# Dynamic convolution into a two-layer tanh-shrink network: a softmax product on another engine, another way of filling the halo and the weights, and another last superblock

## Chip, core and metric

The kernel runs on one core of one Trainium2 chip. The metric is the device time of one execution in microseconds (us), as the median of several runs. The engines are named as in the profile: PE (matmuls), PEld (its weight loads), DVE (vector), ACT (scalar, activations), POOL (GpSimd), SP (issues DMAs).

## What is computed

```python
# x: 8 x 4096 x 192, weight_gen: 8 x 4096 x 8 heads x 7 taps
w = np.exp(weight_gen - max over taps);  w = w / sum over taps
x_pad = six zero rows ahead of each sequence, then x
conv[b, s, h, g] = sum over k of w[b, s, h, k] * x_pad[b, s + k, h, g]    # 24 channels per head
h = conv.reshape(32768, 192) @ w_in        # 192 x 2048
g = h - np.tanh(h)
out = g @ w_out                            # 2048 x 192
```

## The kernel before

The 32768 tokens are cut into 32 superblocks of 1024 tokens, four to a sequence; a superblock puts 8 consecutive tokens (`J`) on each of the 128 partitions. For superblock n the stages are these.

`load(n)` (lines 71 to 105) issues the DMAs on SP: the taps `wg_t`, and `x_t`, which holds for each partition its 8 rows and the 6 rows ahead of them (the halo). In the first superblock of a sequence the halo of partition 0 is zero: DVE writes it with a memset (line 94), and the rows come in three DMAs rather than one.

`softmax_exp(n)` is one ACT instruction (line 110), `e_t`. `softmax_norm(n)` is three on DVE: the sum over taps `zsum` (120), its reciprocal `zr` (124), and the product `wsm` = `e_t` * `zr` (126, 448 elements per partition).

`products(n)` (133) makes seven tiles `prod0` to `prod6`, one per tap, each `x_t` shifted by the tap times that tap's weight (1536 elements per partition). They are on POOL, save in the first two superblocks: DVE makes taps 1, 3, 5, 6 of superblock 0 and taps 2, 5 of superblock 1. Each tap has two buffers.

`conv(n, chunks)` (151) sums the seven products and transposes them, with 64-row matmuls against an identity into `pc`; ACT copies the result to `convT` (174). It is called twice, for channel chunks 0 and 1 and for chunk 2.

`gemm1(n, f)` (182), for each of 16 tiles of the 2048 hidden columns, makes `ph` in PSUM with 12 half-array matmuls per pair of tiles; ACT takes `th` = tanh(`ph`) (196); DVE takes `gt` = `ph` - `th` (198). `ph` and `pc` share three PSUM buffers of two banks each.

`gemm2(i)` (204) makes the output of token block i (8 blocks to a superblock): 16 matmuls on the upper 64 rows of the array for block i and 16 on the lower 64 rows for block i-1, in turns, so that the two halves of one block's sum are made in two successive calls and add up in one bank, `po`. ACT copies `po` to `out_sb` (242); a superblock's output leaves in one DMA.

The order of the program is written out by hand (lines 251 to 297), and every engine runs its own instructions in that order. `w_in` is wanted twice, on partitions 0 to 63 and on 64 to 127: before, 16 DMAs on POOL's queue read it twice from memory (256), then one reads `w_out` (261). Then come the softmax and the products of superblocks 0 and 1, and a loop over n: `products(n+2)`, `load(n+3)`, and for p = 0 to 7 two calls of `gemm1(n)`, one of `gemm2` for superblock n-1, `conv(n+1)` at p = 2 and p = 5, `softmax_exp(n+3)` at p = 1 and `softmax_norm(n+3)` at p = 2. The last trip, n = 32, holds only the `gemm2` calls of superblock 31, and one more call closes the last block.

Of the kernel before, what the change touches and what calls it, by code (L numbers as in the profile page):

```python
# [16 lines left out]
def kernel(  # L17
# [42 lines left out]
    make_identity(nc, ident[:])  # L60

# [3 lines left out]
    wsm_of = {}  # L65
# [5 lines left out]
    def load(n):  # L71
# [21 lines left out]
        if s == 0:  # L93
            nc.vector.memzero(x_t[0:1, 0:HALO, :])  # L94
# [22 lines left out]
    def softmax_norm(n):  # L117
# [6 lines left out]
        nc.vector.reciprocal(zr[:], zsum[:])  # L124
        wsm = wgpool.tile([P, J, H, K], FP32, name="wsm")
        nc.vector.tensor_mul(  # L126
# [4 lines left out]
        wsm_of[n] = wsm  # L131

    def products(n, on_vector=()):
        x_t = x_of.pop(n)
        wsm = wsm_of.pop(n)
# [64 lines left out]

    half = {}
    out_of = {}

    def gemm2(i):

        ops = []
        for r, blk in ((0, i), (1, i - 1)):
            if not 0 <= blk < NTOT * J:
                continue
            n, j = divmod(blk, J)  # L210
            if r == 0:
                half[blk] = psum_o.tile([P, 512], FP32, name="po")
            ops.append((r, n, j, half[blk]))
        for f in range(NFT):
            for r, n, j, po in ops:
# [8 lines left out]
                if r == 1 and f == 0 and i in (1, NTOT * J):  # L224
# [26 lines left out]
    load(0)  # L251

    w_in = const.tile([P, NC, F], BF16, name="w_in")
    for r in range(2):
        for h in range(H):
            nc.gpsimd.dma_start(  # L256
                out=w_in[r * R + h * GC : r * R + (h + 1) * GC],
                in_=moe_w_in[h * G : (h + 1) * G].rearrange("(c g) f -> g c f", c=NC),
            )
    w_out = const.tile([P, NFT, D], BF16, name="w_out")  # L260
    nc.gpsimd.dma_start(out=w_out[:], in_=moe_w_out.rearrange("(c p) e -> p c e", c=NFT))  # L261

    ctx.enter_context(tc.manual_schedule())
# [7 lines left out]
    load(2)  # L271
    conv(0, (0, 1))
    conv(0, (2,))
    products(1, on_vector=(2, 5))
    softmax_exp(2)
    softmax_norm(2)
    for n in range(NTOT + 1):
        if n + 2 < NTOT:
            products(n + 2)
        if n + 3 < NTOT:  # L280
            load(n + 3)
        for p in range(J):
            if n < NTOT:
                gemm1(n, 2 * p)
                gemm1(n, 2 * p + 1)
# [4 lines left out]
            if n + 1 < NTOT:  # L290
                if p == 2:
                    conv(n + 1, (0, 1))
                if p == 5:
                    conv(n + 1, (2,))
            if p == 2 and n + 3 < NTOT:
                softmax_norm(n + 3)
    gemm2(NTOT * J)
# [30 lines left out]
```

## Time and profile before

| what | value |
|---|---|
| median of 3 runs | 861.99 us (861.54 to 863.34) |
| the profiled execution | 862.46 us |
| its span | 860.7 us, so 1.76 us lie around it |
| mean granted clock of PE | 0.984 |
| busy: PE, DVE, ACT, POOL | 779.2, 707.5, 641.3, 644.9 us |

A row of the timeline has a start, a duration, the engine, the line, what is written and read, how many instructions it merges (x4), and in brackets how long the engine was idle before it and who ended that. A row of the windows has a stretch, its length, each engine's busy time (with the number of instructions), the granted clock of PE, the busy share of the DMA engines and GB/s.

### The profile page before, as it was taken

The numbers are of one execution on the slowest core, as the hardware profiler recorded it, in microseconds if no ns is written. First come the engines' busy times: TensorE is split into PE (matmuls) and PEld (weight loads), VectorE is DVE, ScalarE is ACT, GpSimd is POOL, SyncE is SP. The second block draws the span as 40 slices with busy tenths as digits, with TensorE's granted clock in tenths as the row PEclk, the third lists the DMA queues.
The fourth block names the chain that finished last, engine by engine and source line by source line (L and its number), as shares of the span: only waits on it lengthen the run. The fifth ranks groups of instructions, "written<-read, shape, count | busy, mean of one in ns | idle before, by whom it ended". The sixth has DMA issues, their size and how long they took to land.

```text
span 860.7 us, 36095 instructions
## 1 busy us (share of the span) xinstructions
PE 779.2 (91%) x16640; PEld 604.4 (70%) x16640; DVE 707.5 (82%) x622; ACT 641.3 (75%) x865; POOL 644.9 (75%) x241
## 2 busy tenths in 40 slices
PE   0337999989999899999999899998999899999996
PEld 0224877767777677777777677776777677777775
DVE  4397888898888888888888988888888978887790
ACT  1136888868888688878788788887888678888881
POOL 3899888878888688986888699886888788884000
PEclk9978999999999999999999999999999999999999
DMA  9822223331333232233223322332233313200111
GB/s 197 146 77 76 88 93 114 114 113 50 114 115 93 86 115 83 81 115 113 84 97 114 113 64 102 113 114 77 104 113 115 113 51 113 104 11 30 40 39 75
DMA packets 17192, 81.19 MB, mean 94 GB/s; under 512 B 4368, under 2 KB 8464, under 8 KB 12952
## 3 DMA queue, kind: packets, MB, share of 16 engines
q1 hardware_dynamic: 13952, 76.52, 26.8%
q0 software_dynamic: 3088, 2.36, 2.1%
q8 instruction: 130, 2.13, 1.0%
q14 instruction: 22, 0.18, 0.1%
HBM read 56.06 MB, written 25.17 MB: 94 GB/s over the span
## 4 chain that ended last, share of the span: by engine, by line
PE 66%; DVE 21%; ACT 7%; issue 2%; DMA 2%; POOL 2%; DVEq 0%; POOLq 0%
PE po L217 31%; PE ph L187 31%; DVE gt L198 15%; ACT th L196 6%; PE pc L164 4%; DVE wsm L126 4%; DMA w_in<-in_moe_w_in_dram 2%; POOL prod L141 1%; DVE zr L124 1%; DVE zsum L120 1%; POOL w_in L256 1%; ACT out_sb L242 1%; DVE x_t L94 0%; ACT e_t L110 0%; POOL ident masks.py:199 0%
## 5 line engine op out<-in xcount | busy, mean ns | idle before, releaser
L141 POOL TENSOR_TENSOR prod<-x_t,wsm 128x1536 bf16<-128x1536 f32 x218 | 633.6, 2943 | 122.4 <-PE pc L164 121.7
L198 DVE TENSOR_TENSOR gt<-ph,th 128x1024 bf16<-128x1024 f32 x512 | 600.7, 1217 | 101.5 <-ACT th L196 101.3
L196 ACT ACTIVATE th<-ph 128x1024 f32<-128x1024 f32 x512 | 498.2, 1022 | 81.7 <-PE ph L187 79.3
L187 PE MATMUL ph<-convT,w_in 64*128 64x512 bf16 x3072 | 397.1, 381 | 35.4 <-DVE gt L198 31.7
L217 PEld LDWEIGHTS <-gt 64*128 64x128 bf16 x8192 | 359.2, 95 | 57.7 <-issue 5.7
L217 PE MATMUL po<-w_out,gt 64*128 64x192 bf16 x8192 | 390.6, 244 | 4.8 <-ACT out_sb L242 3.8
L187 PEld LDWEIGHTS <-w_in 64*128 64x128 bf16 x3072 | 169.3, 95 | 155.6 <-issue 63.2
L164 PE MATMUL pc<-ident,prod 64*128 64x64 bf16 x5376 | 93.7, 192 | 36.8 <-POOL prod L141 35.0
L164 PEld LDWEIGHTS <-prod 64*128 64x128 bf16 x5376 | 89.8, 96 | 38.2 <-POOL prod L141 35.3
L242 ACT ACTIVATE out_sb<-po 128x192 f32<-128x192 f32 x256 | 85.2, 333 | 39.7 <-PE po L217 36.2
L174 ACT ACTIVATE convT<-pc 128x1024 bf16<-128x1024 f32 x64 | 51.8, 810 | 79.8 <-PE pc L164 79.6
L126 DVE TENSOR_TENSOR wsm<-e_t,zr 128x448 f32<-128x448 f32 x32 | 56.2, 1756 | 2.7
L120 DVE TENSOR_REDUCE zsum<-e_t 128x64 f32<-128x448 f32 x32 | 19.5, 609 | 15.7 <-ACT e_t L110 15.7
L110 ACT ACTIVATE e_t<-wg_t 128x448 f32<-128x448 f32 x32 | 18.4, 575 | 13.4 <-DMA wg_t<-in_weight_gen_dram 13.4
L256 POOL DMA_DIRECT2D w_in<-in_moe_w_in_dram x16 | 9.4, 592 | 15.1 <-DMA w_in<-in_moe_w_in_dram 14.5
L124 DVE RECIPROCAL zr<-zsum 128x64 f32<-128x64 f32 x32 | 17.7, 553 | 1.1
L141 DVE TENSOR_TENSOR prod<-x_t,wsm 128x1536 bf16<-128x1536 f32 x6 | 10.2, 1754 | 9.5 <-DMA x_t<-in_x_dram 9.5
L94 DVE MEMSET x_t<- 1x1152 uint32 x8 | 8.1, 1018 | 2.3 <-PEq L312 1.0
L261 POOL DMA_DIRECT2D w_out<-in_moe_w_out_dram x1 | 1.2, 1203 | 1.3 <-DMA w_in<-in_moe_w_in_dram 1.3
L110 ACT ACT_TABLE_LOAD x1 | 1.3, 1283 | 0.7 <-PEq L312 0.7
masks.py:197 POOL MEMSET ident<- 128x128 bf16 x1 | 0.2, 205 | 0.3 <-POOLq L312 0.3
masks.py:199 POOL TENSOR_SCALAR_AFFINE_SELECT ident<-ident 128x128 bf16<-128x128 bf16 x1 | 0.3, 304 | 0.1
(4 smaller groups left out, 0.4 us busy)
## 6 DMA issues: line engine op xcount, KB each, us to landing
x_t<-in_x_dram SPq DMA_DIRECT2D x24, 1344.0 KB, 7.1
out_dram<-out_sb SPq DMA_DIRECT2D x32, 768.0 KB, 3.8
x_t<-in_x_dram SPq DMA_DIRECT2D x8, 1176.0 KB, 7.0
wg_t<-in_weight_gen_dram SPq DMA_DIRECT2D x32, 224.0 KB, 3.9
w_in<-in_moe_w_in_dram POOLq DMA_DIRECT2D x16, 96.0 KB, 11.9
x_t<-in_x_dram SPq DMA_DIRECT2D x8, 157.5 KB, 3.2
w_out<-in_moe_w_out_dram POOLq DMA_DIRECT2D x1, 768.0 KB, 7.9
x_t<-in_x_dram SPq DMA_DIRECT2D x8, 6.0 KB
```

Source lines behind the costliest of these rows:

```text
L110: nc.scalar.activation(out=e_t[:].rearrange("p j h k -> p (j h k)"), in_=wg_t[:].rearrange("p j h k -> p (j h k)"), func=ACT.Exp,)
L120: nc.vector.reduce_sum(out=zsum[:], in_=e_t[:].rearrange("p j h k -> p (j h) k"), axis=AX.X)
L124: nc.vector.reciprocal(zr[:], zsum[:])
L126: nc.vector.tensor_mul(wsm[:].rearrange("p j h k -> p (j h) k"), e_t[:].rearrange("p j h k -> p (j h) k"), zr[:].rearrange("p (n o) -> p n ...
L141: eng.tensor_mul(prod[:].rearrange("p c j h g -> p j h c g"), x_t[:, k : k + J, :].rearrange("p j (h c g) -> p j h c g", h=H, c=NC), wsm[: ...
L164: nc.tensor.matmul(pc[:, r, col : col + R], lhsT=prods[k][r * R : (r + 1) * R, c, 2 * j : 2 * j + 2].rearrange("p j h g -> p (j h g)"), rh ...
L174: nc.scalar.activation(out=convT[:, c0 : c0 + nch, :].rearrange("p c (j r t) -> p r (c j) t", r=2, t=R), in_=pc[:, :, 0 : nch * JH * R].re ...
L187: nc.tensor.matmul(ph[:, r, :], lhsT=w_in[r * R : (r + 1) * R, c, f * P : (f + 1) * P], rhs=convT[r * R : (r + 1) * R, c, :], start=(c == ...
L196: last_act[0] = nc.scalar.activation(out=th[:], in_=ph_f, func=ACT.Tanh)
L198: nc.vector.tensor_sub(gt[:], ph_f, th[:])
L217: mm = nc.tensor.matmul(po[:, 0:D], lhsT=g_of[n][f][r * R : (r + 1) * R, col : col + P], rhs=w_out[r * R : (r + 1) * R, f, :], start=(r == ...
L242: last_act[0] = nc.scalar.activation(out=out_sb[:, j, :], in_=po[:, 0:D], func=ACT.Copy)
```

## The change

Four edits, and an order that goes with them.

1. **Halo.** A tile `zero` of 192 zeros is made once, and the halo of a sequence's first superblock is filled by a small DMA from it on SP in place of the memset on DVE.
2. **Softmax product.** `wsm` moves from `softmax_norm` on DVE to the head of `products` on POOL; its reads and its result are the same.
3. **w_in.** Eight DMAs read it once into partitions 0 to 63; one DMA on SP copies it to partitions 64 to 127. That copy stands in SP's order ahead of `load(1)` and waits for the eight. `w_out` is read after `products(0)`.
4. **Last superblock.** `gemm2` ends at block 247 (`LAST` = 248). The eight blocks of superblock 31 go through `gemm2_last`: the two row halves of one block are summed in the same call, in two banks of the buffers that `ph` uses; ACT copies one bank, DVE adds the other, and the output leaves in four DMAs of 192 KB.

In the loop `load(n+3)` stands ahead of `products(n+2)`, and `conv(1)` stands at p = 5 and p = 6 of trip 0 (p = 2 and 5 before). `load(2)` stands after `products(1)`.

```diff
         if s == 0:
-            nc.vector.memzero(x_t[0:1, 0:HALO, :])
+            nc.sync.dma_start(
+                out=x_t[0:1, 0:HALO, :],
+                in_=zero[:].rearrange("o (h d) -> o h d", h=1).to_broadcast([1, HALO, D]),
+            )
...
+    def products(n, on_vector=()):
+        x_t = x_of.pop(n)
+        e_t, zr = zr_of.pop(n)
         wsm = wgpool.tile([P, J, H, K], FP32, name="wsm")
-        nc.vector.tensor_mul(
+        nc.gpsimd.tensor_mul(
...
+    def gemm2_last(j):
+        n = NTOT - 1
+        po = psum_h.tile([P, 2, HT], FP32, name="po2", tag="ph")
+        col = (j % 2) * HT + (j // 2) * P
+        for f in range(NFT):
+            for r in range(2):
+                nc.tensor.matmul(
+                    po[:, r, 0:D],
+                    lhsT=g_of[n][f][r * R : (r + 1) * R, col : col + P],
+                    rhs=w_out[r * R : (r + 1) * R, f, :],
+                    start=(f == 0),
+                    stop=(f == NFT - 1),
+                )
...
+        ot = tpool.tile([P, D], FP32, name="ot", tag="th")
+        nc.scalar.activation(out=ot[:], in_=po[:, 0, 0:D], func=ACT.Copy)
+        nc.vector.tensor_add(out_sb[:, j, :], po[:, 1, 0:D], ot[:])
...
     load(0)
+    for h in range(H):
+        nc.gpsimd.dma_start(
+            out=w_in[h * GC : (h + 1) * GC],
+            in_=moe_w_in[h * G : (h + 1) * G].rearrange("(c g) f -> g c f", c=NC),
+        )
     softmax_exp(0)
     softmax_norm(0)
+    products(0, on_vector=(1, 3, 5, 6))
+    nc.sync.dma_start(out=w_in[R:P], in_=w_in[0:R])
     load(1)
-    products(0, on_vector=(1, 3, 5, 6))
+    nc.gpsimd.dma_start(out=w_out[:], in_=moe_w_out.rearrange("(c p) e -> p c e", c=NFT))
```

POOL's instructions at the start of the program, before. The digit behind `prod` is the tap, the number behind `_` tells superblocks apart (`wsm_124` is superblock 0, `wsm_150` superblock 1, `wsm_349` superblock 2); `x15` stands for the other fifteen reads of w_in.

```order
L256 DMA w_in_97<-in_moe_w_in_dram 8x3x2048 x15
L261 DMA w_out_114<-in_moe_w_out_dram 128x16x192
L141 TENSOR_TENSOR prod0_130<-x_t_92,wsm_124 128x64x3x8
L141 TENSOR_TENSOR prod2_134<-x_t_92,wsm_124 128x64x3x8
L141 TENSOR_TENSOR prod4_138<-x_t_92,wsm_124 128x64x3x8
L141 TENSOR_TENSOR prod0_329<-x_t_128,wsm_150 128x64x3x8
L141 TENSOR_TENSOR prod1_331<-x_t_128,wsm_150 128x64x3x8
L141 TENSOR_TENSOR prod3_335<-x_t_128,wsm_150 128x64x3x8
L141 TENSOR_TENSOR prod4_337<-x_t_128,wsm_150 128x64x3x8
L141 TENSOR_TENSOR prod6_341<-x_t_128,wsm_150 128x64x3x8
L141 TENSOR_TENSOR prod0_351<-x_t_154,wsm_349 128x64x3x8
```

The same place of POOL after the change, from behind the last read of w_in (`wsm_117`, `wsm_318` and `wsm_348` are superblocks 0, 1 and 2).

```order
L136 TENSOR_TENSOR wsm_117<-e_t_111,zr_115 128x448
L146 TENSOR_TENSOR prod0_119<-x_t_98,wsm_117 128x64x3x8
L146 TENSOR_TENSOR prod2_123<-x_t_98,wsm_117 128x64x3x8
L146 TENSOR_TENSOR prod4_127<-x_t_98,wsm_117 128x64x3x8
L301 DMA w_out_93<-in_moe_w_out_dram 128x16x192
L136 TENSOR_TENSOR wsm_318<-e_t_139,zr_143 128x448
L146 TENSOR_TENSOR prod0_320<-x_t_136,wsm_318 128x64x3x8
L146 TENSOR_TENSOR prod1_322<-x_t_136,wsm_318 128x64x3x8
L146 TENSOR_TENSOR prod3_326<-x_t_136,wsm_318 128x64x3x8
L146 TENSOR_TENSOR prod4_328<-x_t_136,wsm_318 128x64x3x8
L146 TENSOR_TENSOR prod6_332<-x_t_136,wsm_318 128x64x3x8
L136 TENSOR_TENSOR wsm_348<-e_t_338,zr_342 128x448
```

Eight reads of w_in are gone from ahead of the first product, the read of w_out stands behind the first three, and each superblock's products begin with its `wsm`.

DVE's instructions at the head of trip 1 of the loop, before; this trip loads superblock 4, the first of a sequence, so the memset is there. `gt15` is the last tile of superblock 0, `gt0` the first of superblock 1.

```order
L198 TENSOR_TENSOR gt15_724<-ph_715,th_722 128x1024
L94 MEMSET x_t_742 1x1152
L198 TENSOR_TENSOR gt0_756<-ph_747,th_754 128x1024
L198 TENSOR_TENSOR gt1_767<-ph_758,th_765 128x1024
L198 TENSOR_TENSOR gt2_795<-ph_786,th_793 128x1024
L198 TENSOR_TENSOR gt3_806<-ph_797,th_804 128x1024
L198 TENSOR_TENSOR gt4_854<-ph_845,th_852 128x1024
L198 TENSOR_TENSOR gt5_865<-ph_856,th_863 128x1024
L120 TENSOR_REDUCE zsum_1016<-e_t_808 128x64
L124 RECIPROCAL zr_1018<-zsum_1016 128x64
L126 TENSOR_TENSOR wsm_1020<-e_t_808,zr_1018 128x448
L198 TENSOR_TENSOR gt6_1031<-ph_1022,th_1029 128x1024
```

And after the change, from the same `gt15` to the same `gt6`.

```order
L203 TENSOR_TENSOR gt15_717<-ph_708,th_715 128x1024
L203 TENSOR_TENSOR gt0_751<-ph_742,th_749 128x1024
L203 TENSOR_TENSOR gt1_762<-ph_753,th_760 128x1024
L203 TENSOR_TENSOR gt2_790<-ph_781,th_788 128x1024
L203 TENSOR_TENSOR gt3_801<-ph_792,th_799 128x1024
L203 TENSOR_TENSOR gt4_849<-ph_840,th_847 128x1024
L203 TENSOR_TENSOR gt5_860<-ph_851,th_858 128x1024
L125 TENSOR_REDUCE zsum_1011<-e_t_803 128x64
L129 RECIPROCAL zr_1013<-zsum_1011 128x64
L203 TENSOR_TENSOR gt6_1024<-ph_1015,th_1022 128x1024
```

Two instructions are gone between `gt15` and `gt6`: the memset, which stood in every fourth trip, and `wsm`, which stood in every trip.

More of the change, by code (lines that the diff above doesn't have):

```diff
@@ L60 @@
     make_identity(nc, ident[:])
+    zero = const.tile([1, D], FP32, name="zero")
+    nc.vector.memzero(zero[:])
     x_of = {}
@@ L64 @@
     e_of = {}
-    wsm_of = {}
+    zr_of = {}
     prods_of = {}
@@ L274 @@
     products(1, on_vector=(2, 5))
+    load(2)
     softmax_exp(2)
     softmax_norm(2)
-    for n in range(NTOT + 1):
+    for n in range(NTOT):
+        if n + 3 < NTOT:
+            load(n + 3)
         if n + 2 < NTOT:
             products(n + 2)
-        if n + 3 < NTOT:
-            load(n + 3)
         for p in range(J):
-            if n < NTOT:
-                gemm1(n, 2 * p)
-                gemm1(n, 2 * p + 1)
+            gemm1(n, 2 * p)
+            gemm1(n, 2 * p + 1)
             if p == 1 and n + 3 < NTOT:
@@ L296 @@
                 softmax_norm(n + 3)
-    gemm2(NTOT * J)
+    gemm2(LAST)
+    for j in range(J):
+        gemm2_last(j)
 _INS = ['x', 'weight_gen', 'moe_w_in', 'moe_w_out']
```

38 lines of the change are left out of this document (19 added, 19 removed).

## Prediction

> **What bounds the kernel now.** I read the windows first, one for each round of four superblocks (a sequence), from the same pair of `gt` instructions to the same pair.
>
> ```profile
> 143.25:243.14 99.89, 96.74 (x2086) 75.43 (x2082) 86.35 (x77) 79.87 (x109) 81.41 (x28) 0.98 0.29 98
> ...
> 638.69:739.36 100.67, 97.17 (x2086) 75.75 (x2082) 86.71 (x78) 79.87 (x109) 81.40 (x28) 0.98 0.30 99
> 739.36:810.82 71.46, 71.18 (x1566) 55.68 (x1562) 58.54 (x52) 59.04 (x80) 40.51 (x14) 1.00 0.12 49
> sum 667.57, PE 648.27 PEld 504.72 DVE 577.20 ACT 538.28 POOL 528.95; mean PE 92.61 PEld 72.10 DVE 82.46 ACT 76.90 POOL 75.56
> ```
>
> The last row is three superblocks, 23.82 us each, with PE busy in 71.18 of 71.46 us: there PE is the bound, and nothing in the change touches its work. The seven rows hold 27 superblocks; at 23.82 us they would take 643.1 us, and they take 667.6. So 24.4 us is waiting, about 4 in each full round. The DVE timeline shows a plain superblock and then the one of the round that waits.
>
> ```profile
> 160.96 1.05 DVE L126 TENSOR_TENSOR wsm<-e_t,zr 128x448 f32<-128x448 f32 x1
> ...
> 175.91 1.02 DVE L94 MEMSET x_t<- 1x1152 uint32 x1 [0.18 <-PE po L217]
> 176.86 4.54 DVE L198 TENSOR_TENSOR gt<-ph,th 128x1024 bf16<-128x1024 f32 x4
> ...
> 185.44 3.25 DVE L126 TENSOR_TENSOR wsm<-e_t,zr 128x448 f32<-128x448 f32 x1
> ```
>
> PE answers in the same place:
>
> ```profile
> 178.06 0.82 PE L187 MATMUL ph<-convT,w_in 64*128 64x512 bf16 x6 [0.55 <-DVE gt L198]
> ...
> 185.57 1.50 PE L217 MATMUL po<-w_out,gt 64*128 64x192 bf16 x32
> 186.89 0.83 PE L187 MATMUL ph<-convT,w_in 64*128 64x512 bf16 x6
> 189.88 0.82 PE L187 MATMUL ph<-convT,w_in 64*128 64x512 bf16 x6 [2.17 <-DVE gt L198]
> 190.53 2.65 PE L217 MATMUL po<-w_out,gt 64*128 64x192 bf16 x32
> ```
>
> The memset delays `gt` by a microsecond and PE waits 0.55 us; then `wsm` takes 3.25 us and PE waits 2.17 us for the next `gt`; after that the same 32 matmuls take 2.65 us instead of 1.50, the clock having dropped. Why `wsm` takes so long is in POOL's rows beside the spread of `wsm`.
>
> ```profile
> L126 DVE TENSOR_TENSOR wsm<-e_t,zr x32: 624/1048/9317, 5.5 to 757.1; 128x448 f32<-128x448 f32 x32
> 168.16 20.06 POOL L141 TENSOR_TENSOR prod<-x_t,wsm 128x1536 bf16<-128x1536 f32 x7 [3.38 <-PE pc L164]
> L141 POOL TENSOR_TENSOR prod<-x_t,wsm x218: 2892/2902/3293, 28.4 to 781.4; 128x1536 bf16<-128x1536 f32 x109
> ```
>
> POOL's seven products run from 168.16 to 188.22 at 2.87 us each; the seventh starts at 185.36, just ahead of `wsm`, and `wsm` ends 0.47 us behind it, where it takes 0.62 undisturbed. Both read two tiles in SBUF, and DVE's waits until POOL's is through. The starting stage shows more:
>
> ```profile
> 24.14 3.43 DVE L141 TENSOR_TENSOR prod<-x_t,wsm 128x1536 bf16<-128x1536 f32 x2 [0.98 <-DMA x_t<-in_x_dram]
> 42.44 9.32 DVE L126 TENSOR_TENSOR wsm<-e_t,zr 128x448 f32<-128x448 f32 x1
> 51.68 3.47 DVE L198 TENSOR_TENSOR gt<-ph,th 128x1024 bf16<-128x1024 f32 x3
> ...
> 60.51 3.35 DVE L126 TENSOR_TENSOR wsm<-e_t,zr 128x448 f32<-128x448 f32 x1
> ...
> 72.08 4.62 DVE L198 TENSOR_TENSOR gt<-ph,th 128x1024 bf16<-128x1024 f32 x4 [0.84 <-ACT th L196]
> ```
>
> ```profile
> 27.13 1.20 POOL L261 DMA_DIRECT2D w_out<-in_moe_w_out_dram  x1 [1.27 <-DMA w_in<-in_moe_w_in_dram]
> 28.35 22.92 POOL L141 TENSOR_TENSOR prod<-x_t,wsm 128x1536 bf16<-128x1536 f32 x8
> 51.89 40.85 POOL L141 TENSOR_TENSOR prod<-x_t,wsm 128x1536 bf16<-128x1536 f32 x14 [0.62 <-issue]
> ```
>
> At 42.44 DVE asks, and gets in only when POOL's chain of eight ends at 51.27: it was passed over at three boundaries between POOL instructions. All of trip 0 stands behind that.
>
> **Steady state: memset and wsm leave DVE.** Both causes of the 24.4 us go. What stays are a few short waits in `conv` for nothing the profile shows:
>
> ```profile
> 336.19 0.30 PE L164 MATMUL pc<-ident,prod 64*128 64x64 bf16 x9 [0.25 <-issue]
> ```
>
> Three such rows, in superblocks 0.4 us longer than the others, make 1.1 us: gain 23.3 us. The cover for `wsm` on POOL is POOL's own idle time, 3.38 us a superblock in the row at 168.16, ahead of the first product, where it waits for PE to free a buffer; `wsm` waits for nothing there, since `zr` was made a trip earlier. Its price on POOL is in no row. From below: 448/1536 of a product, 0.85 us; from above, a whole product, 2.9 us. I take 1.0, nearest the lower end, since a product's time is mostly its elements. Even 2.9 gives 20.06 + 2.9 = 23.0, under 23.82. The zero DMA goes on SP's queue, beside the load that already waited there; I cost it at nothing, and if it delayed `x_t` by 2 us there would still be a trip between its landing and its products.
>
> **Start.** The first `x_t` landed at 14.6 and the competing reads of `w_in` up to there are the same eight, so it lands at 14.6 again.
>
> ```profile
> 14.62 6.76 DVE L141 TENSOR_TENSOR prod<-x_t,wsm 128x1536 bf16<-128x1536 f32 x4 [8.52 <-DMA x_t<-in_x_dram]
> ```
>
> Before, DVE's four products ran alone, and POOL's came at 28.35, behind sixteen DMA issues. Now POOL's three (8.6 us) and DVE's four (6.8) want SBUF together; one after the other they end at 30.0 (POOL's third ended at 37.0 before). Then come DVE's `zsum` and `zr` of superblock 1 or POOL's issue of `w_out` (the row at 27.13), 1.2 us either way:
>
> ```profile
> L120 DVE TENSOR_REDUCE zsum<-e_t 128x64 f32<-128x448 f32 x32 | 19.5, 609 | 15.7 <-ACT e_t L110 15.7
> ...
> L124 DVE RECIPROCAL zr<-zsum 128x64 f32<-128x64 f32 x32 | 17.7, 553 | 1.1
> ```
>
> With `wsm`, 1.0, superblock 1's products may start at 32.3, if its `x_t` is there. That load now stands behind the w_in copy on SP:
>
> ```profile
> 15.28 1.16 POOL L256 DMA_DIRECT2D w_in<-in_moe_w_in_dram  x2 [0.18 <-issue]
> ...
> 24.71 1.16 POOL L256 DMA_DIRECT2D w_in<-in_moe_w_in_dram  x2 [2.64 <-DMA w_in<-in_moe_w_in_dram]
> ```
>
> These POOL issues each wait for an earlier read: by 15.3 four of the first eight had landed, by 24.7 all, with the second `x_t` competing. Without it I take 18. Then copy, taps and `x_t` (0.79 + 0.22 + 1.34 MB) at the 197 GB/s of the first slice of the span:
>
> ```profile
> GB/s 197 146 77 76 88 93 114 114 113 50 114 115 93 86 115 83 81 115 113 84 97 114 113 64 102 113 114 77 104 113 115 113 51 113 104 11 30 40 39 75
> ```
>
> 12 us, so 30: in time. With 24.7 it would be 36.7, 4.4 late.
>
> At 32.3 DVE's two and POOL's five products become ready together, and who goes first decides the size of the gain.
>
> ```profile
> 54.45 1.02 ACT L196 ACTIVATE th<-ph 128x1024 f32<-128x1024 f32 x1 [10.44 <-PE ph L187]
> ```
>
> ```profile
> 55.50 1.23 DVE L198 TENSOR_TENSOR gt<-ph,th 128x1024 bf16<-128x1024 f32 x1 [0.35 <-ACT th L196]
> ```
>
> I take DVE: this `gt` follows its `th` by 0.03 us, while POOL's row at 51.89 began 0.13 behind the end of the `wsm` it waited for (51.76); and I take it that DVE's chain holds on as POOL's did, since its rows too overlap (two take 3.43 us and four 6.76, so each further one adds 1.67, while one lasts 1.76). Then DVE is through at 35.7 and begins `gt` at 37 (before 51.68). POOL makes its five by 50.1, `wsm` by 51.1, the seven of superblock 2 by 71.2, and `conv(2)` in trip 1 ends at 71.5. Before, it ended at 88.3:
>
> ```profile
> 86.50 1.81 PE L164 MATMUL pc<-ident,prod 64*128 64x64 bf16 x110
> ```
>
> DVE's side: trip 0 took from 51.68 to 76.70, 25.0, less the 3.35 of `wsm`, plus 1 for `conv(1)` late in the trip: done at 59.7; from there to the end of `conv(2)` 11.6 less the memset, 70.3. POOL is the later by a microsecond. Gain 16.8 us.
>
> **End.** Before, each of nine calls waits for the copy of the bank that the last one filled:
>
> ```profile
> 839.32 1.50 PE L217 MATMUL po<-w_out,gt 64*128 64x192 bf16 x32 [0.42 <-ACT out_sb L242]
> ...
> 854.64 1.49 PE L217 MATMUL po<-w_out,gt 64*128 64x192 bf16 x16 [0.42 <-ACT out_sb L242]
> 856.17 0.33 ACT L242 ACTIVATE out_sb<-po 128x192 f32<-128x192 f32 x1 [1.58 <-PE po L217]
> ```
>
> Now nothing waits: one closing call at 839.32 and eight at the steady pitch of 1.32 us (185.57 to 186.89), so 839.32 + 9 x 1.32 + 0.2 = 851.4, against 856.1: 4.7 us. A DVE add of 192 elements comes behind the copy, and the last DMA is 192 KB, not 768:
>
> ```profile
> L198 DVE TENSOR_TENSOR gt<-ph,th 128x1024 bf16<-128x1024 f32 x512 | 600.7, 1217 | 101.5 <-ACT th L196 101.3
> ...
> out_dram<-out_sb SPq DMA_DIRECT2D x32, 768.0 KB, 3.8
> ...
> x_t<-in_x_dram SPq DMA_DIRECT2D x8, 157.5 KB, 3.2
> ```
>
> From `gt`, 1217 ns for 1024 elements, and the undisturbed `wsm`, 624 for 448, an element costs 1.03 ns and an instruction 0.16 us, so the add some 0.36 us, an estimate. I take 1.1 off the last one's 4.2 (856.5 to 860.7; bounds 0 and 2). Gain 4.7 - 0.36 + 1.1, so 5.5 us.
>
> **The sum.** 23.3 + 16.8 + 5.5 = 45.6 from the profiled execution's 862.46 gives 816.9; that execution is 0.5 above the median, so 816.4; I say 817.
>
> **A rule, and what it would give.** The Trainium skill, "SBUF — State Buffer", section "Who interferes with whom", says that a DVE instruction with two SBUF inputs and a reading GpSimd instruction share one port under an exclusive lock, held for one instruction, and that the order of issue decides who blocks. The trace agrees on the lock, and disagrees on its length: 9.32 us is three POOL instructions and more.
>
> **Rivals.** (a) POOL goes first at 32.3, or slips in behind DVE's first product. Its chain of five holds DVE for 14.3 us, as the row at 42.44 has it; `gt` begins at 32.3 + 14.3 + 3.4 + 1.2 = 51.2, trip 0 ends at 73.9, `conv(2)` at 84.5: start gain 3.8, total 829.4. For it: the only row with both engines asking shows POOL keeping the port. Against it: there POOL was first.
> (b) The engines take turns, instruction by instruction (what the skill's wording gives): `gt` from 39.8, `conv(2)` by DVE at 73.1, 1.6 later than forecast, 818. Against it: those three boundaries.
> (c) The waits in the rounds were not DVE's but come back at another place: no 23.3, so 840. Against it: both PE rows name `gt`.
> (d) Slower: POOL becomes the bound. Above `wsm` = 3.76 us a superblock takes 20.06 + `wsm`; from there each microsecond costs 30, and the 45.6 are used up at 5.3 us; at 6 the time is 883. Against it: 448 elements would have to cost more than a product of 1536. The skill's "GPSIMD Engine Reference", section 4.1, does speak against the move, with two-input work about twice as slow as on VectorE; by its figure for 2048 elements I estimate 0.98 us, far under that point.
>
> **Chances and range.** Forecast 0.48, (a) 0.32, (b) 0.10, (c) 0.05, (d) 0.02, the rest 0.03 between them. The forecast's own range is 811 to 823: the pairs at 14.6 overlapping after all takes up to 6 off, a late `x_t` adds up to 4.4, the end is worth 1 either way. With (a) at 829 and its own 4 us the range is 811 to 833. A measurement of this kernel tells 0.2% from no change. Faster by more than that 0.97, within it 0.01, slower 0.02.
>
> **What would show it.** Right: rounds of 95.3 to 96 us, `wsm` on POOL at about 1 us and no PE wait for `gt` in them, `gt` from 37, `conv(2)` done by 72, nine calls without gaps at the end. Wrong: a DVE product of 14 us or more at 32 (then (a)); a POOL without idle time in the rounds (then (d)).

## The result, and the profile after

The changed kernel takes 822.0 us (median of four runs, 820.17 to 822.5), against 861.76 us (860.19 to 863.34) for the kernel before on the same chip: a ratio of 0.9535, 95% interval 0.9511 to 0.9558. The profiled execution took 822.47 us with a span of 820.7. Forecast were 817 and the range 811 to 833. Two executions further down that took far longer than the others of their kernel (2839.03 us of start alone, 1032.85 us of end alone) are left out of the medians and ratios.

To see where the 40.0 us of the two spans came from, I cut both at the same two instructions: the first row of the second part of `conv` of superblock 2 (rows at 96.23 before and 78.88 after), and the first closing `gemm2` call that waits for a copy (839.32 and 804.81).

| stretch | before | after | gain | forecast |
|---|---|---|---|---|
| start, to `conv(2)`'s second part | 96.23 | 78.88 | 17.35 | 16.8 |
| rounds, from there to the closing call | 743.09 | 725.93 | 17.16 | 23.3 |
| end | 21.38 | 15.89 | 5.49 | 5.5 |

Start and end came as forecast. The rounds fell 6.1 us short.

**The rounds.** The windows of the changed kernel, cut at the second part of `conv` in each fourth superblock (the last two rows are three superblocks, and the two that come ahead of all these):

```profile
130.07:225.33 95.26, 94.89 (x2086) 74.17 (x2082) 79.67 (x73) 79.64 (x109) 88.40 (x35) 1.00 0.33 111
225.33:322.05 96.72, 95.45 (x2085) 75.83 (x2082) 79.66 (x73) 79.86 (x109) 83.97 (x32) 1.00 0.31 105
...
705.56:777.00 71.44, 71.17 (x1566) 55.64 (x1562) 57.58 (x51) 59.03 (x80) 41.05 (x15) 1.00 0.11 43
78.88:130.07 51.19, 48.05 (x1046) 38.44 (x1042) 39.83 (x37) 39.82 (x55) 51.03 (x20) 1.00 0.30 97
sum 698.12, PE 690.11 PEld 542.33 DVE 575.42 ACT 577.04 POOL 600.35; mean PE 86.26 PEld 67.79 DVE 71.93 ACT 72.13 POOL 75.04
```

The same 29 superblocks of the kernel before:

```profile
96.23:143.95 47.72, 47.45 (x1046) 37.12 (x1042) 41.72 (x39) 39.83 (x55) 40.90 (x14) 1.00 0.29 103
143.95:811.51 667.56, 648.26 (x14045) 504.71 (x14042) 577.20 (x514) 538.27 (x728) 528.95 (x182) 0.99 0.28 94
```

The 27 superblocks of the forecast went from 667.56 to 698.12 - 51.19 = 646.93 us, a gain of 20.6 for 23.3. The two superblocks ahead of them got slower: 47.72 to 51.19, a loss of 3.5. The granted clock is 1.00 in every row, so it is no part of that. `wsm` on POOL is not the reason either; it costs what the forecast took:

```profile
L136 POOL TENSOR_TENSOR wsm<-e_t,zr 128x448 f32<-128x448 f32 x32 | 31.1, 972 | 1.7 <-DVE zr L129 1.7
```

What is left in PE's timeline of the changed kernel, after superblock 2, are waits that the profile calls "issue", nine rows with 5.28 us (before there were seven with 2.00, none longer than 0.58 and none ahead of 312):

```profile
101.53 1.15 PE L223 MATMUL po<-w_out,gt 64*128 64x192 bf16 x23 [1.92 <-issue]
121.00 1.21 PE L169 MATMUL pc<-ident,prod 64*128 64x64 bf16 x71 [0.97 <-issue]
255.67 0.32 PE L223 MATMUL po<-w_out,gt 64*128 64x192 bf16 x3 [0.16 <-issue]
289.82 1.45 PE L192 MATMUL ph<-convT,w_in 64*128 64x512 bf16 x11 [0.33 <-issue]
313.92 0.27 PE L169 MATMUL pc<-ident,prod 64*128 64x64 bf16 x7 [0.43 <-issue]
361.98 0.51 PE L169 MATMUL pc<-ident,prod 64*128 64x64 bf16 x23 [0.30 <-issue]
386.25 0.62 PE L169 MATMUL pc<-ident,prod 64*128 64x64 bf16 x31 [0.40 <-issue]
639.56 0.32 PE L223 MATMUL po<-w_out,gt 64*128 64x192 bf16 x3 [0.29 <-issue]
697.42 0.27 PE L169 MATMUL pc<-ident,prod 64*128 64x64 bf16 x7 [0.48 <-issue]
```

The longest of the seven before:

```profile
373.46 0.81 PE L187 MATMUL ph<-convT,w_in 64*128 64x512 bf16 x5 [0.58 <-issue]
```

No `gt`, no `wsm` and no memset ends a wait there any more. The two longest rows lie in the two superblocks that got slower. Timed from one second part of `conv` to the next, 19 of the 29 superblocks take 23.81 or 23.82 us; the other ten, nine of which hold these rows, take 7.5 us more in all. So a row costs more than its idle time, by 0.1 to 0.5 us, and these waits are nearly all that the rounds are above 23.82 us a superblock.

**The start.** DVE, then POOL, in the timeline of the changed kernel, and the spread of DVE's products in the view of the tile:

```profile
14.67 14.88 DVE L146 TENSOR_TENSOR prod<-x_t,wsm 128x1536 bf16<-128x1536 f32 x4 [9.65 <-DMA x_t<-in_x_dram]
31.82 6.13 DVE L146 TENSOR_TENSOR prod<-x_t,wsm 128x1536 bf16<-128x1536 f32 x2 [1.15 <-POOL wsm L136]
38.98 3.42 DVE L203 TENSOR_TENSOR gt<-ph,th 128x1024 bf16<-128x1024 f32 x3
```

```profile
14.70 13.24 POOL L146 TENSOR_TENSOR prod<-x_t,wsm 128x1536 bf16<-128x1536 f32 x3 [7.16 <-DMA x_t<-in_x_dram]
31.86 17.43 POOL L146 TENSOR_TENSOR prod<-x_t,wsm 128x1536 bf16<-128x1536 f32 x5
50.30 20.06 POOL L146 TENSOR_TENSOR prod<-x_t,wsm 128x1536 bf16<-128x1536 f32 x7
```

```profile
L146 DVE TENSOR_TENSOR prod<-x_t,wsm x6: 1757/4452/4458, 14.7 to 33.5; 128x1536 bf16<-128x1536 f32 x6
```

A product of DVE takes 1.76 us where it goes first and 4.45 where a POOL product (2.7 more) comes ahead of it. Three on POOL and four on DVE, begun together at 14.7, end at 27.9 and 29.55: here the engines take turns, one instruction each. Then the five and the two of superblock 1 do the same. POOL is done with them at 49.3 and with superblock 2 at 70.4, and `conv(2)` follows:

```profile
69.14 1.81 PE L169 MATMUL pc<-ident,prod 64*128 64x64 bf16 x110
...
78.88 1.00 PE L169 MATMUL pc<-ident,prod 64*128 64x64 bf16 x56
```

**The end.** One call waits, the eight others run without a gap, and the add is as short as estimated:

```profile
804.81 1.24 PE L223 MATMUL po<-w_out,gt 64*128 64x192 bf16 x13 [0.42 <-ACT out_sb L248]
...
806.08 10.78 PE L264 MATMUL po<-w_out,gt 64*128 64x192 bf16 x253
```

```profile
817.26 0.36 DVE L276 TENSOR_TENSOR out_sb<-po,ot 128x192 f32<-128x192 f32 x1 [0.96 <-ACT ot L275]
```

### The profile page after: what moved, and what is told of

Same layout as the page of the kernel before. It is cut to its first block, busy times and chain, and to the rows that moved or that the text cites. A ratio compares the mean times of both kernels' runs of the same rounds, so it can differ in the third digit from the quotient of the medians.

```text
span 820.7 us, 35994 instructions
## 1 busy us (share of the span) xinstructions
PE 769.5 (94%) x16640; PEld 602.6 (73%) x16640; DVE 661.0 (81%) x591; ACT 640.1 (78%) x865; POOL 669.0 (82%) x265
## 3 DMA queue, kind: packets, MB, share of 16 engines
q8 instruction: 130, 2.13, 1.1%
## 4 chain that ended last, share of the span: by engine, by line
PE 79%; DVE 13%; ACT 4%; issue 2%; DMA 1%; SPq 0%; POOL 0%; ACTq 0%; DVEq 0%; POOLq 0%
PE ph L192 36%; PE po L223 35%; DVE gt L203 10%; PE pc L169 6%; ACT th L201 4%; DVE prod L146 3%; DMA x_t<-in_x_dram 1%; PE po L264 1%; DVE zr L129 0%; DVE zsum L125 0%; POOL wsm L136 0%; SPq L96 0%; ACT e_t L115 0%; SPq L100 0%; SPq L77 0%
## 5 line engine op out<-in xcount | busy, mean ns | idle before, releaser
L192 PE MATMUL ph<-convT,w_in 64*128 64x512 bf16 x3072 | 393.1, 378 | 13.8 <-DVE gt L203 10.5
L192 PEld LDWEIGHTS <-w_in 64*128 64x128 bf16 x3072 | 171.3, 94 | 128.5 <-issue 38.1
L248 ACT ACTIVATE out_sb<-po 128x192 f32<-128x192 f32 x248 | 82.5, 333 | 24.3 <-PE po L223 20.7
L136 POOL TENSOR_TENSOR wsm<-e_t,zr 128x448 f32<-128x448 f32 x32 | 31.1, 972 | 1.7 <-DVE zr L129 1.7
L146 DVE TENSOR_TENSOR prod<-x_t,wsm 128x1536 bf16<-128x1536 f32 x6 | 21.0, 3556 | 10.8 <-DMA x_t<-in_x_dram 9.6
L276 DVE TENSOR_TENSOR out_sb<-po,ot 128x192 f32<-128x192 f32 x8 | 2.9, 357 | 8.9 <-ACT ot L275 8.9
L275 ACT ACTIVATE ot<-po 128x192 f32<-128x192 f32 x8 | 2.6, 330 | 7.9 <-PE po L264 7.9
L292 POOL DMA_DIRECT2D w_in<-in_moe_w_in_dram x8 | 4.8, 604 | 0.4 <-issue 0.4
```

The lines of the kernel that those rows point to most:

```text
L136: nc.gpsimd.tensor_mul(wsm[:].rearrange("p j h k -> p (j h) k"), e_t[:].rearrange("p j h k -> p (j h) k"), zr[:].rearrange("p (n o) -> p n ...
L146: eng.tensor_mul(prod[:].rearrange("p c j h g -> p j h c g"), x_t[:, k : k + J, :].rearrange("p j (h c g) -> p j h c g", h=H, c=NC), wsm[: ...
L192: nc.tensor.matmul(ph[:, r, :], lhsT=w_in[r * R : (r + 1) * R, c, f * P : (f + 1) * P], rhs=convT[r * R : (r + 1) * R, c, :], start=(c == ...
L248: last_act[0] = nc.scalar.activation(out=out_sb[:, j, :], in_=po[:, 0:D], func=ACT.Copy)
```

## The experiments

The table has the stretches of each profiled execution, cut as above, the sum of PE's "issue" waits in the rounds, and the ratio to the kernel before on the same chip. The stretches are those of one execution and the ratio is that of all, and the two can differ: halo alone was profiled at 842.89 us with a median of 845.41, start alone at 853.46 with 855.85, the kernel before at 862.46, where its median on the chip that ran the four parts is 858.98.

| kernel | start | rounds | waits | end | ratio (95%) |
|---|---|---|---|---|---|
| before | 96.23 | 743.09 | 2.00 | 21.38 | 1 |
| halo alone | 92.62 | 727.12 | 3.18 | 21.36 | 0.9854 (0.9821 to 0.9887) |
| `wsm` alone | 106.46 | 725.73 | 1.88 | 21.41 | 0.9946 (0.9928 to 0.9963) |
| start alone | 88.21 | 741.59 | 1.84 | 21.80 | 0.9964 (0.9946 to 0.9983) |
| end alone | 93.36 | 741.18 | 1.81 | 15.96 | 0.9932 (0.9910 to 0.9953) |
| all (the change) | 78.88 | 725.93 | 5.28 | 15.89 | 0.9535 (0.9511 to 0.9558) |
| stores apart | 78.78 | 725.87 | 3.99 | 15.85 | 0.9554 (0.9530 to 0.9578) |
| stores meet | 78.46 | 724.25 | 3.55 | 15.89 | 0.9568 (0.9541 to 0.9596) |
| `x_t` in halves | 81.69 | 725.64 | 3.43 | 15.87 | 0.9586 (0.9563 to 0.9609) |
| POOL first | 80.53 | 724.04 | 3.62 | 15.83 | 0.9571 (0.9548 to 0.9594) |
| no loads of `x` | 80.44 | 721.43 | 1.43 | 15.63 | 0.9520 (0.9491 to 0.9550) |
| 64 matmuls ahead | 79.95 | 727.53 | 6.48 | 15.82 | 0.9602 (0.9568 to 0.9635) |
| DVE asks late | 81.52 | 723.47 | 3.22 | 15.91 | one run |
| `conv` in thirds | 77.10 | 724.20 | 3.06 | 15.90 | 0.9541 (0.9513 to 0.9569) |

In the nine kernels from "all" on, the rounds less the waits come to 720.0 to 722.2 us: what differs in their rounds is for the most part the waits.

### One part alone

**Halo alone**: the kernel before with line 94 replaced.

```diff
-            nc.vector.memzero(x_t[0:1, 0:HALO, :])
+            nc.sync.dma_start(out=x_t[0:1, 0:HALO, :], in_=zero[:]...to_broadcast([1, HALO, D]))
```

> The halo edit alone: zeros by DMA, all else as before (wsm stays on DVE). Theory: in the rounds the wait needs two things together, the memset that pushes wsm later by a microsecond and POOL's seventh product that starts in that microsecond; without the memset every wsm falls where it does in the plain superblocks (about 1.05 us) and the six waiting rounds go, some 20 us: 842. Rival: wsm alone makes the long wait and the memset only its own 0.6 to 0.7 us of PE time in six rounds: 858.

845.41 us. The rounds give 16.0 of the 17.2 that the whole change gives, though `wsm` stays on DVE: without the memset ahead of it, it comes a little sooner and gets in before POOL's last product (1.05 us, as in a plain superblock), not behind it. DVE's timeline of this kernel:

```profile
42.09 9.32 DVE L131 TENSOR_TENSOR wsm<-e_t,zr 128x448 f32<-128x448 f32 x1
...
60.10 0.63 DVE L131 TENSOR_TENSOR wsm<-e_t,zr 128x448 f32<-128x448 f32 x1
...
277.67 2.76 DVE L131 TENSOR_TENSOR wsm<-e_t,zr 128x448 f32<-128x448 f32 x1
```

In the rounds it is long twice (277.67 and 663.40), each time 11 us behind an "issue" wait of PE (0.92 us at 266.72, 0.81 at 652.46) that made DVE late, and PE then waits 1.75 and 1.87 us for `gt`. Those two waits are what halo alone keeps; `wsm` alone, the next run, keeps five of 0.54 to 0.55 us behind the memset. So in the rounds memset and `wsm` were for the most part one cause of waiting, not two.

**`wsm` alone**: line 126 goes to POOL, at the head of `products`.

```diff
-        nc.vector.tensor_mul(
+        nc.gpsimd.tensor_mul(
```

> The softmax product alone on POOL; the memset stays, w_in is read twice on POOL's queue as before. Theory: in the rounds only the memset's 0.7 us times six stays, so 17 us are gained there; at the start wsm of superblock 0 now stands behind sixteen reads of w_in on POOL, so DVE's first four products wait until 29 and nothing is gained there: about 844 (start between 3 us better and 5 worse). Rival: the memset is what counts in the rounds, then 5 us at most: 857.

854.68 us, nearer the rival's number, but not for its reason. The theory is right for the rounds, which give 17.4, and wrong for the start, which is 10.2 longer where it allowed 5. POOL's first `wsm` now stands behind the sixteen reads of `w_in` on POOL's queue, and DVE's products wait for it; and the memset of superblock 4 waits for POOL's products of superblock 2, with `gt` behind it on DVE:

```profile
30.46 14.89 DVE L141 TENSOR_TENSOR prod<-x_t,wsm 128x1536 bf16<-128x1536 f32 x4 [24.99 <-POOL wsm L131]
...
86.46 1.02 DVE L94 MEMSET x_t<- 1x1152 uint32 x1 [5.54 <-POOL prod L141]
```

PE waited 6.00 us for the `gt` behind that memset. With the other edits neither delay is there: POOL's first `wsm` stands behind eight reads (at 6.56), and no memset waits for POOL.

**Start alone**: `w_in` read once and copied, and the new order of the start and the loop.

> The order of the start alone: w_in read once and copied, w_out behind the first products, loads and conv(1) placed as in the changed kernel; wsm and the memset stay on DVE, the last superblock as before. Rounds unchanged. Theory (DVE and POOL take turns at the port, instruction by instruction): wsm of superblock 2 waits for one POOL product at most, gt begins at about 41, conv(2) ends at about 75: 13 us less, 849. Rival (a chain of POOL products holds the port to its end, as at 42.44 in the kernel before): wsm of superblock 2 gets in at 48.5, gt begins at 49, conv(2) ends at 83: 5 us less, 857.

855.85 us, nearer the rival's 857 than the theory's 849. The start of the profiled execution is 8.0 shorter (2.9 of that is chance, see end alone), the rounds wait as before, and `conv(2)` ends at 79.1, between the two forecasts (75 and 83). The order of the engines is the theory's all the same; the rival's chains do not appear. DVE's timeline:

```profile
12.70 14.89 DVE L141 TENSOR_TENSOR prod<-x_t,wsm 128x1536 bf16<-128x1536 f32 x4 [6.39 <-DMA x_t<-in_x_dram]
...
36.75 2.02 DVE L126 TENSOR_TENSOR wsm<-e_t,zr 128x448 f32<-128x448 f32 x1
```

The `wsm` of superblock 2, 9.32 us before, gets in at POOL's next boundary here.

**End alone**: `LAST` and `gemm2_last`.

> The last superblock alone, summed from two banks. Theory: nine waits of 0.42 us go, the pitch falls from 1.92 to 1.32 us, the last DMA is shorter: 5.5 us less, 856.3. Rival: the copies or the DVE adds set the pitch instead, so that only the shorter last DMA is left: 1 us less, 861.

853.37 us against 858.98 before on that chip, 5.6 less, and 5.4 in the end of the trace: additive, since nothing else hangs on it. A by-product: its start is the old one, yet 2.9 shorter than in the profile of before, since the `wsm` of superblock 3, 3.35 us there, took 0.63 (as in halo alone). That much of the start's 17.35 is a chance of one profiled execution.

By their ratios the four parts alone save 12.5, 4.6, 3.1 and 5.8 us, 26 in all, and together 40. One reason stands in the rows: the start that `wsm` alone lengthens by 10.2 us is not lengthened in the whole.

### What the waits of PE are

Two runs were to move the stores, which I suspected of meeting the loads:

```diff
+                late.append((n, out_sb))
+                if not (n <= 2):      # the other kernel: n <= NTOT - 3
+                    store()
...
+            if p == 3 and late:       # the other kernel: p == 5
+                store()
```

> The changed kernel, with the output stores of superblocks 0, 1 and 2 issued three steps of the loop later, so that they no longer fall on the load of x_t (in the changed kernel they are issued 0.4, 2.1 and 6 us behind it). Theory: PE waits for its instructions, which come by DMA and stand behind these bursts; the waits of 1.92 us at 101.5 and 0.97 us at 121.0 go, with what they cost beside themselves 3.2 us: 818.8. Rival: those waits have another cause: no change, 822.

> The changed kernel, with the output store of every superblock but the last two issued five steps later, so that each falls on a load of x_t. Theory: PE's instructions stand behind a burst of 2.3 MB in nearly every superblock; waits of 1 to 2 us each in some 25 of them, 25 to 50 us more: 847 to 872. Rival (the waits have nothing to do with these transfers): within 1 us of 822.

820.84 and 821.72 us, and neither theory was tested. SP runs ahead of the other engines and issues a store as soon as its data is there (the first at 91.84 in the changed kernel, at 91.82 and 91.43 in these two); between the old and the new place of the store stands no other issue on SP, so its queue is the same in both kernels. The two are repeats of the changed kernel, and useful as that: ratios of 0.9554 and 0.9568 beside 0.9535, rounds of 725.9 and 724.3, and the wait at 121.00 absent in both. Differences of this size below say nothing.

**`x_t` in halves**: each load of `x_t` in two DMAs of 7 rows.

> The changed kernel, with each load of x_t in two DMAs of 7 rows, so that each run in a partition is 5376 B instead of 10752. Theory in a stronger form (the DMA engines take a piece from each queue in turn, so that smaller pieces of x_t let PE's instructions through sooner): most of the 7 us of waits for nothing shown go, 3 to 6 us less: 816 to 819. Rival in the theory (only the bytes ahead count): no change, 822.

824.01 us. The first load landed at 17.5 and not at 14.7, the start is 2.8 longer, and the rounds are the same. The 816 to 819 of the theory is missed, and the rival's "no change" holds for the rounds.

**No loads of `x`** from superblock 5 on:

```diff
+        if n > 4:
+            wg_of[n] = wg_t
+            x_of[n] = kept[n % 2]
+            return
```

> The changed kernel with the loads of x from superblock 5 on left out: those superblocks use the window of an older superblock again, so the output is not the reference's; everything else is issued as before. The question is what the PE waits marked 'issue' of the changed kernel hang on (nine rows with 5.3 us, 7.5 us of loop time over 29 superblocks at 23.8). Theory 'instructions behind loads': PE's own instructions are brought in by DMA, 16 KB or 256 of them at a time; PE runs through 224 of them in the 1.6 us of conv's first part, and where the next 16 KB are asked for there while a 1.3 MB load of x lies in the DMA engines, PE waits. Then the rows after about 130 us (255.7, 289.8, 313.9, 362.0, 386.3, 639.6, 697.4) are gone, the loop comes to 29 times 23.8 plus the two early waits, and the time to 816 to 818. Rival 'conv alone': PE is through conv faster than any instructions can follow, load or no load; then the rows stay within 0.1 us of their size and the time is 822.

817.56 us, and 1.43 us of waits for 5.28. All that is left of them in PE's timeline:

```profile
287.65 1.45 PE L199 MATMUL ph<-convT,w_in 64*128 64x512 bf16 x11 [0.26 <-issue]
311.66 0.27 PE L176 MATMUL pc<-ident,prod 64*128 64x64 bf16 x7 [0.35 <-issue]
359.59 0.51 PE L176 MATMUL pc<-ident,prod 64*128 64x64 bf16 x23 [0.22 <-issue]
383.76 0.62 PE L176 MATMUL pc<-ident,prod 64*128 64x64 bf16 x31 [0.30 <-issue]
670.68 1.45 PE L199 MATMUL ph<-convT,w_in 64*128 64x512 bf16 x11 [0.30 <-issue]
```

The time is the theory's, but each side has a part. The two long early waits and three of the later ones (255.67, 639.56 and 697.42) are gone with the loads; four stay at their places, a little shorter, without any load, and one at 670.68 is new.

**64 matmuls ahead**: 128 more PE instructions while PE has nothing to do.

```diff
+    shift = psum_o.tile([P, 512], FP32, name="po")
+    for i in range(64):
+        nc.tensor.matmul(shift[:, 0:16], lhsT=ident[:], rhs=ident[:, 0:16], start=(i == 0), stop=(i == 63))
```

> The changed kernel with 64 matmuls of 16 columns on the identity ahead of everything on PE, in the 30 us in which PE has nothing to do: 128 more PE instructions, and nothing else moved. A superblock has 1,040 PE instructions, 16 more than four times 256, so the places at which a stretch of 256 ends move by 16 instructions each superblock, and 128 more at the start put them where they are eight superblocks (190.5 us) away in the changed kernel. Theory 'instructions': the waits move by 190 us: those near 255.7, 289.8, 313.9, 362.0, 386.3, 639.6 and 697.4 go, and waits of 0.2 to 0.5 us come near 446, 480, 504, 552, 577 and perhaps near 65 to 195; the time is within 2 us of 822. Rival 'transfers': the waits hang on where loads and stores lie, which nothing here moves; then they stay at their places, at 822.

825.21 us, outside the 2 us that was allowed: the start is 1.1 us longer and the waits of the rounds 1.2. PE's timeline (three rows of 0.58, 0.17 and 0.45 us, at 96.68, 171.55 and 196.31, are left out):

```profile
123.55 0.27 PE L169 MATMUL pc<-ident,prod 64*128 64x64 bf16 x7 [3.21 <-issue]
...
449.84 0.32 PE L223 MATMUL po<-w_out,gt 64*128 64x192 bf16 x3 [0.50 <-issue]
483.99 1.45 PE L192 MATMUL ph<-convT,w_in 64*128 64x512 bf16 x11 [0.34 <-issue]
508.12 0.27 PE L169 MATMUL pc<-ident,prod 64*128 64x64 bf16 x7 [0.47 <-issue]
556.34 0.51 PE L169 MATMUL pc<-ident,prod 64*128 64x64 bf16 x23 [0.33 <-issue]
580.64 0.62 PE L169 MATMUL pc<-ident,prod 64*128 64x64 bf16 x31 [0.43 <-issue]
```

Set beside the changed kernel's rows: the same instructions (x3, x11, x7, x23, x31), in the same order, each 194.2 to 194.4 us later, and nothing left at 255, 290, 314, 362 or 386. The loads did not move by 194 us. The waits go with the count of PE's instructions, and the page shows the unit:

```profile
PE 769.5 (94%) x16640; PEld 602.6 (73%) x16640; DVE 661.0 (81%) x591; ACT 640.1 (78%) x865; POOL 669.0 (82%) x265
...
q8 instruction: 130, 2.13, 1.1%
```

2 x 16,640 instructions of PE are 130 times 256, and q8 brings in 130 packets of 2.13/130 MB, 16 KB each. A superblock has 1,040 instructions, 16 more than four packets, so the boundary wanders through it, and the 128 extra ones put it eight superblocks away.

The trace also keeps the time of each packet, and that ties every wait to one of them. Counted from the program's first matmul, the nine rows of the changed kernel begin at matmuls 1245, 1629, 4573, 5341, 5853, 6877, 7389, 12893 and 14173. Each of these leaves 93 when divided by 128, and a matmul with its weight load is two instructions. So it is in all ten kernels with the new order of the start; in the four with the old one the remainder is 91. These are 91 waits in 14 traces, and no "issue" wait of PE's matmuls lies anywhere else. Each ends 2.2 to 2.8 us after a packet of q8 began.

What makes a wait short or long can be read there too. For the row at 313.92 the packet began at 311.33, 0.5 us after PE had passed the boundary before (310.81); but PE had run through the 256 instructions between, 210 of them of `conv`, in 2.7 us, and waited 0.43. For the row at 101.53 PE passed the boundary before at 93.99, and the packet began only at 99.11, 5.1 us later. SP had issued a load of `x_t` at 91.45 and a store at 91.84, and until the packet began the DMA engines were full with queue q1. The first line is queue q1 from 94 to 99, where q8 has no packet; the second is q8 from 99.1 to 99.2:

```profile
q1 hardware_dynamic: 193, 1.50, 97.8%
...
q8 instruction: 1, 0.02, 60.3%
```

The 3.21 us at 123.55 has both causes: 2.7 us for the 256 instructions, and a packet that began 3.5 us after the boundary before, behind a load and a store issued at 113.57 and 113.98. Without the loads of `x` (the run before) no such long wait is left. Whether the load alone would do it, without the store, no run shows.

The Trainium skill, "Runtime: NRT & Kernel Launch", section "Instruction fetch mechanics", says that an engine's instructions are brought in by its own DMA queue in blocks of 16 KiB, 256 instructions, and that crossing a block is mostly hidden since instructions are issued more slowly than they are brought in. The unit agrees; the hiding holds for most of the 130 boundaries and fails here where PE has run through 224 instructions of `conv` in 1.63 us, or where the packet begins late.

**`conv` in thirds**, and the memset for superblock 0 alone:

```diff
-                if p == (2 if n else 5):
-                    conv(n + 1, (0, 1))
-                if p == (5 if n else 6):
-                    conv(n + 1, (2,))
+                if n and p in (2, 3, 5):
+                    conv(n + 1, ((2, 3, 5).index(p),))
```

> The changed kernel with conv of superblocks 2 on in three parts of 56 matmuls (after the pairs of f tiles 2, 3 and 5) for one of 112 and one of 56, and with the six zero rows of superblock 0 alone by a memset on DVE again, so that its load of x is not issued behind the DMA of zeros. Theory 'instructions': a stretch of 256 PE instructions that lies in conv now lasts 3.8 us or more for 2.1, so the next one has time to come and the PE waits of the loop (7.5 us) go, all but 1 to 2 us; ScalarE gets one more eviction, 0.17 us more a superblock in time in which it waits for PE; the first load lands 1 to 2 us earlier and takes as much from the start: 813 to 816. Rival 'the waits come back elsewhere' (the third part takes a third bank pair in turn, or the waits aren't from conv's pace): the loop stays at 7 us over or gains waits on ScalarE, and only the start's 1 to 2 us are had: 820 to 821.

819.43 us, between the two forecasts. The short waits of `conv` are gone; three rows stay. They are the changed kernel's rows at 101.53, 121.00 and 255.67, all of which went with the loads of `x`:

```profile
99.23 1.15 PE L226 MATMUL po<-w_out,gt 64*128 64x192 bf16 x23 [1.63 <-issue]
118.97 0.39 PE L172 MATMUL pc<-ident,prod 64*128 64x64 bf16 x15 [1.25 <-issue]
253.97 0.32 PE L226 MATMUL po<-w_out,gt 64*128 64x192 bf16 x3 [0.18 <-issue]
```

That answers to the theory, but the size does not: rounds of 724.2 us are no better than those of "stores meet", a repeat of the changed kernel. The start is 1.8 shorter. The span is the shortest of all, while the ratio cannot be told from that of the changed kernel, so I cannot call it faster.

### Who gets the port

**POOL first**: POOL's five products of superblock 1 and the work of `load(2)` to `softmax_norm(2)` stand ahead of DVE's two.

> The changed kernel, with DVE's two products of superblock 1 behind its zsum and zr of superblock 2, so that POOL's chain of five has begun (31.9) when DVE asks (34.2). Theory (turns): DVE gets in at POOL's next boundary, its first product takes at most 4.5 us, gt begins at about 42, and the end moves by 2 to 4 us: 824 to 826. Rival (who is first keeps the port for its chain): DVE's first product takes 12 us or more, gt begins at 49.5, the end is 9 to 12 us later: 831 to 834.

822.22 us. DVE asks at 33.88, 2 us into POOL's chain, and gets in at the next boundary; its two take 6.78 us for 6.13. So the turns are as the theory has them, and its 824 to 826 is missed: `gt` began at 40.58 and not at 42. The second part of `conv(2)` begins 1.65 later, and the rounds' waits happen to be smaller by as much.

**DVE asks late**: the same, with the first two evictions of `gemm1` ahead of DVE's two as well.

> The changed kernel with DVE's two products of superblock 1 put behind the first two evictions of gemm1, so that DVE asks near 39.5 us, when GpSimd has run its own five products for some 8 us undisturbed (they begin near 31.9 and take 2.8 us each alone: ends near 34.7, 37.5, 40.4, 43.2 and 46.0). Theory 'a long chain shuts out': as with the scaling of superblock 2 in the kernel before (asked at 42.4, passed over at three ends, 9.3 us), DVE gets in only when the chain is through, near 46.0, and its two products take 9 to 10 us together. Rival 'turns at any time': DVE gets in at the next end, near 40.4, the two products take 5 to 7 us, and GpSimd's chain ends near 49 as in the changed kernel. GpSimd's work to the end of the products of superblock 2 is the same in both, so the time is 821 to 824 in both; the rows tell.

822.65 us in one run. DVE and POOL:

```profile
36.76 7.46 DVE L148 TENSOR_TENSOR prod<-x_t,wsm 128x1536 bf16<-128x1536 f32 x2
```

```profile
32.46 17.38 POOL L148 TENSOR_TENSOR prod<-x_t,wsm 128x1536 bf16<-128x1536 f32 x5
```

DVE asked sooner than meant, at 36.76, 4.3 us into the chain, and was in at the next boundary, the chain's second (32.46 + 2 x 2.8 = 38.1): 1.3 + 1.76 + 4.45 is the 7.46 of the row. Turns again. POOL's five take 17.4 us whichever way the turns fall, so POOL, and with it `conv(2)`, is done at the same distance from the start of the chain.

## Why the prediction was right, and where it failed

- **Start: right in size, wrong in one step.** "DVE's chain holds on as POOL's did" fell: rival (b) is what happens, in the changed kernel, in start alone, in POOL first and in DVE asks late. `gt` began at 38.98, between the forecast's 37 and the 39.8 of (b), and `conv(2)` ended at 71.0 for 71.5. The size held because POOL is the later engine there, and its total is the sum of both engines' products in whatever order. Of the gain of 17.35 us, 2.9 are luck: the profiled execution of before lost them by chance (end alone). Luck, too, is the landing of the first load, below.

  The evidence for turns was in the trace of before. The forecast calls the row at 42.44 the only one with both engines asking, but its own rows of `wsm` at 60.51 and 160.96 are others. At 60.51 DVE waited for one product and got in, while POOL's row goes on to 92.7. At 160.96 it got in ahead of the seventh product of this chain, 16.6 us after its start:

```profile
144.33 20.45 POOL L141 TENSOR_TENSOR prod<-x_t,wsm 128x1536 bf16<-128x1536 f32 x7 [3.38 <-PE pc L164]
```

  Of the 30 `wsm` rows before that began while POOL ran products, 23 got in between two products at the next boundary, six came behind a chain's last product, and one is the row at 42.44. So 0.32 was too much for rival (a), which needs POOL's chain to shut DVE's products out (no run showed that), and 0.10 too little for (b).
- **Rounds: the mis-sized term.** The causes were right: memset and `wsm` are gone from every wait. The failed step is "three such rows ... make 1.1 us: gain 23.3 us". The forecast leaves 743.09 - 24.4 = 718.7 us and 1.1 of waits; measured are 720.7 and 5.28. So 4.2 of the 6.1 us are PE's waits for its instructions, and the other 2 stand in the same superblocks, since each wait costs more than its idle time. A round of four superblocks takes 95.2 to 96.8 us, where 95.3 to 96 was the sign of being right. I had taken three short rows as a constant of the kernel, while before's own trace held seven, and their number and size hang on where boundaries and loads fall; the new start brought 2.9 us of them to two superblocks that had none. Without loads of `x` the rounds come to 721.4.
- **`wsm` on POOL: right**, 0.97 us for 1.0 (0.62 on DVE undisturbed), inside POOL's idle time. The advice of the Trainium skill, "GPSIMD Engine Reference", section 4.1, against two-input work there decides nothing here: without the memset the rounds are 727.1 us with `wsm` on DVE (halo alone) and 725.9 with it on POOL (the change). Dear was only the place on the queue, in `wsm` alone.
- **Halo DMA: right** in the rounds, where it costs nothing, and wrong at the very start, where the first load of `x_t` stands behind it: landing 14.67, where start alone and `conv` in thirds, with the memset there, have 12.70 and 12.32. The forecast's "lands at 14.6 again" was met because the DMA that it costed at nothing took about the 2 us that fewer reads of `w_in` gave.
- **End: right** in each piece: no wait but the 0.42 us of the closing call, 1.32 us a call, an add of 0.36, and 3.1 us from the add to the end for 4.2 less 1.1.
- **Rivals (c) and (d):** of (c) a small part holds: 3.3 us more of PE's waits, though of another cause, not the 23.3 in another place. Of (d) nothing: POOL keeps 2.8 us of idle time a superblock.

## What to carry to other kernels

When a trace shows two delays on one engine in the same round, ask whether the second exists only because of the first; here either edit alone brought 16 to 17 of the 17.2 us in its profiled execution, and only the traces of both alone show it. An edit that is cheap where it lands can be dear by what stands ahead of it on that queue. And when the bounding engine is busy 99% of the time, its waits without a releaser are a term of their own: count all of them, and ask what sets their place and size before taking them as constant.

## What the runs showed of the hardware

- PE waits for its own instructions at boundaries of 256, 0.15 to 0.97 us in most of the rows with such a wait and up to 3.21. The wait ends 2.2 to 2.8 us after the packet began. It appears where most of the 256 instructions before the boundary are of `conv` (2.7 us for all of them at 313.92), or where the packet began late behind loads (3.5 to 5.1 us after the boundary before, at 123.55 and 101.53).
- A DVE and a POOL instruction with two SBUF inputs each exclude one another for one instruction and then take turns: 4.45 us for a DVE product of 1.76 beside POOL's, and a `wsm` of 0.62 us that got in at POOL's next boundary 23 times before. The prediction set the 9.32 us row against the Trainium skill's lock of one instruction ("SBUF — State Buffer", section "Who interferes with whom"); in every other row here the page is borne out.
- One thing stays open. The `wsm` of superblock 2 in the kernel before was passed over at three boundaries of POOL (9.32 us; also in halo alone and end alone), at 42 us, 14 us into a chain that nothing had interrupted. The length of the chain is not the reason: at 160.96 the same instruction got in at the next boundary, 16.6 us into a chain that nothing had interrupted either. DVE asks late, which was to try the long chain, asked after 4.3 us. No run shows what sets this one row apart.
